# Retention with a Mish feed-forward layer: state products and scores on quarters of the TensorE array, in one stretch a visit

## The chip, the cores and the metric

The kernel runs on one core of a Trainium2 chip. The metric is the device time of one execution, in microseconds. A profile is of one execution; its span is the time from the first to the last instruction that the profiler saw on the core.

## What is computed

Eight batches of eight heads, 576 positions, head size 64. Each head is a masked product with decay, with no softmax; the heads are then put side by side and go through a two-layer network:

```python
scores = (1/sqrt(64)) * q @ k.T                   # [8, 8, 576, 576]
gamma  = 1 - 2.0 ** (-5 - head)
ret    = (scores * where(i >= j, gamma ** (i - j), 0)) @ v
x      = ret, heads side by side                  # [4608, 512]
h      = x @ w_in                                 # [4608, 2048]
out    = (h * tanh(softplus(h))) @ w_out          # [4608, 512], Mish between
```

## The kernel before

**Chunks and tiles.** The 576 positions of a batch are cut into chunks of 128 (c = 0 to 3) and one of 64; the 64-row ends of two batches make one chunk together (c = 4). The 36 chunks are taken four at a time: nine tiles of 512 tokens. Tiles 0 and 1 hold the chunks with c = 0, which need no state from earlier positions (the functions with f_). The other 28 chunks (numbers 8 to 35, N0 = 8) use the decay's recurrent form. In each:

- P (L271, VectorE) scales q, V (L276, GpSimd) scales v and makes vs; both round to bf16.
- T (L282) turns q and k into qkT, with eight TensorE transposes and a ScalarE copy for chunks below 18 (NPE), by a transposing transfer on SP's queue from 18 on.
- S (L294) makes the scores k q of the chunk with itself, eight matmuls with 64 rows of the array (one head each) and all 128 columns, into two PSUM banks (sc); VectorE multiplies by the causal mask and writes sm.
- state (L319) adds k times v of one chunk of one batch to the PSUM bank st, where the state of a batch is summed over c; VectorE copies it to ssb. Two heads lie above each other in 128 partitions, and the copy writes it twice, each time with the other head's half multiplied by zero (diag), so that the product can use all 128 rows. There are 32 states, in a fixed order; state_of says which one a chunk needs, done counts them, and a call of state makes the next one only if a chunk up to its argument needs it.
- O (L343, step_o) makes the chunk's result: eight products of ssb with q (L353; sixteen where c = 4, since the two 64-token ends need two batches' states) and eight outputs of vs with sm (L358), all of them with 64 columns of the array, added up in one bank (half of sc, or ops in tile 2). VectorE copies it to xT.

**The network.** g1(t, f) (L366 on) makes one of 16 slices of h for tile t: four matmuls of 512 columns at L371 into a bank hp, then Mish on ScalarE into gT. g2(t, i) makes a quarter of the sum of one 128-token result (four matmuls at L386, in a bank ops or hp); after four of them the result waits in ready until stores copies it (L422, VectorE) and sends it off on SP's queue.

**Order.** It is written out by hand, and every engine takes its instructions in program order. The loop over u (L529) runs g1 of tile 1 and the first half of its g2, with chunks 8 to 11 between; then the loop over t and i (L563) runs g1 of tile t and g2 of tile t-1 in turns (16 steps a tile), with two chunks' work in each block of eight steps, w = 0 to 7. In the trace a block shows two stretches of small matmuls: states and S at w = 0, states and O at w = 4. TensorE's last work is g2_last.

**Loads.** All loads are issued from GpSimd's queue (q, k, v with 256-byte runs; w_in and w_out in four loads each), in order with GpSimd's own operations; load (L253) is called by more_loads at w = 4 and 5, some seven chunks ahead of use. Buffers: qraw 5, vraw 7, qks 9, vs 5, sm 3, qkT 5, ssb 6. PSUM has eight banks: sc two times two, st one, hp two, ops one.

## Time and profile before

| | |
|---|---|
| median of three runs | 312.5 us (312.32, 312.5, 315.58) |
| the profiled execution | 313.61 us, span 311.9 us |
| granted TensorE clock | 1.0 of full speed |
| L371 and L386 of 128x512, mean of one | 380 and 379 ns from start to end |
| ScalarE Mish, L373, 128x512 | 598 ns |
| VectorE: sm L305, ssb L336, xT L362, res L422 | 1215, 685, 680, 688 ns |
| GpSimd: one load issue L263 (128 partitions), L267 (64) | 906 to 910, 706 to 745 ns |

TensorE busy, by stage:

| from, us | to, us | what runs | TensorE busy, us |
|---|---|---|---|
| 0 | 20 | first loads, tile 0's chunks | 13.7 of 20.0 |
| 20 | 50.8 | network of tile 0, tile 1's chunks | 30.5 of 30.8 |
| 50.8 | 80.3 | the loop over u | 29.2 of 29.5 |
| 80.3 | 107.2 | t = 2 | 26.6 of 26.8 |
| 107.2 | 262.5 | t = 3 to 7 | 154.2 of 155.3 |
| 262.5 | 294.7 | t = 8 | 32.1 of 32.3 |
| 294.7 | 311.9 | last quarters, store | 14.0 of 17.2 |

How to read it: "busy" counts a matmul from its start to its modelled end, and successive ones overlap; so the distance from start to start tells more than the duration. In a timeline the columns are start and duration in us, engine, line, operation, output and inputs, the array's rows and columns in use (128*64), the size, and how many were merged (x8); in square brackets, how long the engine had been idle and what ended it.

### The profile page before, as it was taken

The numbers are of one execution on the slowest core, as the hardware profiler recorded it, in microseconds if no ns is written. First come the engines' busy times: TensorE is split into PE (matmuls) and PEld (weight loads), VectorE is DVE, ScalarE is ACT, GpSimd is POOL, SyncE is SP. The second block draws the span as 40 slices with busy tenths as digits, with TensorE's granted clock in tenths as the row PEclk, the third lists the DMA queues.
The fourth block names the chain that finished last, engine by engine and source line by source line (L and its number), as shares of the span: only waits on it lengthen the run. The fifth ranks groups of instructions, "written<-read, shape, count | busy, mean of one in ns | idle before, by whom it ended". The sixth has DMA issues, their size and how long they took to land.

```text
span 311.9 us, 5809 instructions
## 1 busy us (share of the span) xinstructions
PE 300.3 (96%) x2429; PEld 152.3 (49%) x2468; DVE 137.1 (44%) x200; ACT 110.7 (36%) x183; POOL 143.6 (46%) x178
## 2 busy tenths in 40 slices
PE   7769999999999999999999999999999999999995
PEld 3444554555465554545454444545454544444444
DVE  4723455778637635443434453535354332001111
ACT  4546345671453623233333333232323333333300
POOL 8578849989985976274726262612010000000000
PEclk9999999999999999999999999999999999999999
DMA  7999999999995999999996949371504100010031
GB/s 177 234 206 205 220 208 221 256 171 175 232 203 96 148 181 191 155 195 146 179 178 116 189 88 218 77 144 37 101 36 101 36 34 36 35 34 34 36 101 68
DMA packets 73642, 42.85 MB, mean 137 GB/s; under 512 B 58640, under 2 KB 64528, under 8 KB 73616
## 3 DMA queue, kind: packets, MB, share of 16 engines
q0 software_dynamic: 48640, 27.27, 61.1%
q1 hardware_dynamic: 24832, 15.08, 23.3%
q8 instruction: 19, 0.31, 0.5%
q10 hardware_dynamic: 144, 0.13, 0.1%
q14 instruction: 7, 0.06, 0.1%
HBM read 38.80 MB, written 9.44 MB: 155 GB/s over the span
## 4 chain that ended last, share of the span: by engine, by line
PE 92%; issue 2%; DMA 2%; POOL 2%; DVE 0%; ACT 0%; POOLq 0%; ACTq 0%
PE hp L371 39%; PE ops L386 30%; PE hp L386 4%; PE sc L301 3%; PE st L333 3%; DMA gT<-in_v_dram 2%; PE hp L403 2%; PE sc L353 2%; PE sc L358 2%; PE sc L288 1%; PE st L403 1%; PE ops L403 1%; PE hp L414 1%; POOL gT L106 1%; POOL vb L222 1%
## 5 line engine op out<-in xcount | busy, mean ns | idle before, releaser
L371 PE MATMUL hp<-xT,w_in_t 128*128 128x512 bf16 (+1 forms) x562 | 141.3, 373 | 2.2 <-DVE xT L239 0.8
L373 ACT ACTIVATE gT<-hp 128x512 bf16<-128x512 f32 (+1 forms) x148 | 86.8, 586 | 156.4 <-PE hp L371 144.2
L386 PE MATMUL ops<-w_out_t,gT 128*128 128x512 bf16 x430 | 110.1, 379 | 0.4
L371 PEld LDWEIGHTS <-w_in_t 128*128 128x128 bf16 x592 | 55.1, 98 | 61.9 <-DVE xT L239 1.3
L386 PEld LDWEIGHTS <-gT 128*128 128x128 bf16 x496 | 48.2, 98 | 58.1 <-issue 0.8
L422 DVE COPY res<-ops 128x512 f32<-128x512 f32 x28 | 19.3, 688 | 82.7 <-PE ops L386 79.7
L279 POOL TENSOR_TENSOR vs<-vraw,gv 128x512 bf16<-128x512 f32 x28 | 30.3, 1096 | 51.8 <-PE sc L358 37.6
L336 DVE TENSOR_TENSOR ssb<-st,diag 128x512 bf16<-128x512 f32 x32 | 21.9, 685 | 47.2 <-PE st L333 47.2
L305 DVE TENSOR_TENSOR sm<-sc,mask 128x1024 bf16<-128x1024 f32 x28 | 33.0, 1215 | 6.2 <-PE sc L301 6.2
L263 POOL DMA_DIRECT2D qraw<-in_q_dram x24 | 21.8, 910 | 12.8 <-DVE qks L273 9.6
L263 POOL DMA_DIRECT2D vraw<-in_v_dram x24 | 21.8, 908 | 2.9 <-DMA vpair<-in_v_dram 1.5
L263 POOL DMA_DIRECT2D qks<-in_k_dram x24 | 21.8, 906 | 1.3 <-DMA w_out_t<-in_moe_w_out_dram 0.9
L273 DVE TENSOR_TENSOR qks<-qraw,gq 128x512 bf16<-128x512 f32 x28 | 20.2, 758 | 0.0
L362 DVE CAST xT<-sc 128x512 bf16<-128x512 f32 x24 | 15.3, 680 | 0.0
L386 PE MATMUL hp<-w_out_t,gT 128*128 128x512 bf16 x61 | 14.7, 379 | 0.2
L289 ACT COPY qkT<-sc 128x1024 bf16<-128x1024 bf16 x10 | 10.1, 1010 | 8.0 <-PE sc L288 8.0
L215 DVE TENSOR_TENSOR sm<-sc,dmask 128x1024 bf16<-128x1024 f32 x8 | 9.4, 1220 | 5.0 <-PE sc L211 5.0
L353 PE MATMUL sc<-qkT,ssb 128*64 128x128 bf16 (+1 forms) x224 | 9.5, 213 | 0.0
L358 PE MATMUL sc<-sm,vs 128*64 128x128 bf16 x192 | 9.4, 219 | 0.0
L301 PE MATMUL sc<-qkT 64*128 64x128 bf16 x224 | 9.0, 218 | 0.0
L403 PEld LDWEIGHTS <-gT 128*128 128x128 bf16 x64 | 5.8, 98 | 6.5
L267 POOL DMA_DIRECT2D qraw<-in_q_dram x8 | 5.6, 706 | 7.3 <-DVE qks L273 7.3
(103 smaller groups left out, 192.0 us busy)
## 6 DMA issues: line engine op xcount, KB each, us to landing
out_dram<-res SPq DMA_DIRECT2D x31, 256.0 KB, 3.0
qraw<-in_q_dram POOLq DMA_DIRECT2D x24, 256.0 KB, 6.0
vraw<-in_v_dram POOLq DMA_DIRECT2D x24, 256.0 KB, 6.8
qks<-in_k_dram POOLq DMA_DIRECT2D x24, 128.0 KB, 6.4
w_in_t<-in_moe_w_in_dram POOLq DMA_DIRECT2D x4, 512.0 KB, 11.1
w_out_t<-in_moe_w_out_dram POOLq DMA_DIRECT2D x4, 512.0 KB, 9.8
gT<-in_q_dram SPq DMA_DIRECT2D x4, 256.0 KB, 4.9
gT<-in_k_dram POOLq DMA_DIRECT2D x8, 128.0 KB, 6.3
```

Of the source, the lines that this page charges most:

```text
L263: nc.gpsimd.dma_start(out=t, in_=src[b, :, ds(P * c, P), :].rearrange("h p d -> p h d"))
L273: nc.vector.tensor_tensor(live[n]["qks"][:, 0], live[n]["q"], gq[:, c, :].unsqueeze(2).to_broadcast([P, H, D]), op=OP.mult)
L279: nc.gpsimd.tensor_tensor(vs, live[n]["v"], gv[:, c, :].unsqueeze(2).to_broadcast([P, H, D]), op=OP.mult)
L301: nc.tensor.matmul(sc[:, e, p, :], lhsT=qk[r, 1, p, :], rhs=qk[r, 0, p, :], start=True, stop=True)
L305: nc.vector.tensor_tensor(sm.rearrange("p e n i -> p (e n) i"), sc.rearrange("p e n i -> p (e n) i"), m.unsqueeze(1).to_broadcast([P, 2 * ...
L336: nc.vector.tensor_tensor(ssb.rearrange("p e n d -> p e (n d)"), st.rearrange("p n d -> p (n d)").unsqueeze(1).to_broadcast([P, 2, NP * 64 ...
L353: nc.tensor.matmul(ot[ds(64 * e, 64), p, ds(i0, iw)], lhsT=st_sb[bb, cc][:, e, p, :], rhs=qk[:, 0, p, ds(i0, iw)], start=(i0 == 0 and p == ...
L371: nc.tensor.matmul(hp[:, cols], lhsT=w_in_t[:, c, ts(f, P)], rhs=xts[t][:, c, cols], start=(c == 0), stop=(c == KC - 1))
L373: nc.scalar.activation(gts[t][:, f, cols], hp[:, cols], AX.Mish)
L386: nc.tensor.matmul(ops, lhsT=gts[t][:, f, ts(s, P)], rhs=w_out_t[:, f, :], start=(f == 0), stop=(f == nF - 1))
L403: nc.tensor.matmul(outs[0, s], lhsT=gts[0][:, f, ts(s, P)], rhs=w_out_t[:, f, :], start=(f == 0), stop=(f == nF - 1))
L422: copy(ot, ops)
```

## The change

- **Scores** use quarters of the array: each head's eight matmuls become sixteen, with 64 rows and 64 columns.
- **States** are copied to ssb once, without zeros (half on VectorE and half on ScalarE from tile 2 on, `two`), and their **products** use 64 rows and 64 columns too.
- So that a quarter's column half goes with a half of the heads, heads h and h+4 now lie above each other in xT, and the rows of w_in are taken in that order, with two loads of 64 partitions in place of each load of 128.
- **One stretch a visit**: two chunks are taken together. A visit makes a state, the outputs of both chunks, a further state, the products, and the scores of the next two chunks. The results lie in two banks, copied to xT by ScalarE and VectorE. A block of eight steps has one visit, at w = 6; the loop over u has a first stretch at u = 9 and visits at 15 and 22, where it had five stretches.
- From tile 3 on the order of g1 and g2 in four steps is g1 g1 g2, g2, g1 g2, g1 g2 (g2 first right after a visit).
- P, V and T come at other steps; for chunks from 18 on, P at w = 4 and 5, T at w = 7 and 0.
- **hold**: before GpSimd issues a block's loads, it copies one element a partition of the qkT of the two chunks whose transposing transfers came last, and so waits for them.

The diff, without its context and without the removed step_o (L343 to L362):

```diff
@@ -79,11 +79,12 @@
-    w_in_r = moe_w_in.rearrange("(c p) f -> p c f", p=P)
+    w_in_r = moe_w_in.rearrange("(a c r) f -> a r c f", a=2, r=64)
     def load_w_in(f0, n):
-        nc.gpsimd.dma_start(out=w_in_t[:, :, ds(f0, n)], in_=w_in_r[:, :, ds(f0, n)])
+        for a in range(2):
+            nc.gpsimd.dma_start(out=w_in_t[ds(64 * a, 64), :, ds(f0, n)], in_=w_in_r[a, :, :, ds(f0, n)])
@@ -156,11 +157,6 @@
-    diag = consts.tile([P, 2], F32)
-    nc.vector.memset(diag, 0.0)
-    nc.vector.memset(diag[0:64, 0:1], 1.0)
-    nc.vector.memset(diag[64:P, 1:2], 1.0)
@@ -231,11 +227,11 @@
-        for p in range(NP):
-            for e in range(2):
-                nc.tensor.matmul(ot[ds(64 * e, 64), p, :], lhsT=vb[:, 2 * p + e, :],
-                                 rhs=fst[t]["sm", b][:, 2 * p + e, :],
-                                 start=(p == 0), stop=True, skip_group_check=True)
+        for h in range(NP):
+            for a in range(2):
+                nc.tensor.matmul(ot[ds(64 * a, 64), h, :], lhsT=vb[:, NP * a + h, :],
+                                 rhs=fst[t]["sm", b][:, NP * a + h, :],
+                                 start=(h == 0), stop=True, skip_group_check=True)
@@ -297,9 +293,10 @@
         for p in range(NP):
             for e in range(2):
-                r = ds(64 * e, 64)
-                nc.tensor.matmul(sc[:, e, p, :], lhsT=qk[r, 1, p, :], rhs=qk[r, 0, p, :],
-                                 start=True, stop=True)
+                for a in range(2):
+                    r, j = ds(64 * e, 64), ds(64 * a, 64)
+                    nc.tensor.matmul(sc[j, e, p, :], lhsT=qk[r, 1, p, j], rhs=qk[r, 0, p, :],
+                                     start=True, stop=True, skip_group_check=True)
@@ -316,7 +313,7 @@
-    def state(upto):
+    def state(upto, two=False):
@@ -332,34 +329,65 @@
-        ssb = tr.tile([P, 2, NP, 64], BF16, name="ssb", bufs=6)
-        nc.vector.tensor_tensor(
-            ssb.rearrange("p e n d -> p e (n d)"),
-            st.rearrange("p n d -> p (n d)").unsqueeze(1).to_broadcast([P, 2, NP * 64]),
-            diag.unsqueeze(2).to_broadcast([P, 2, NP * 64]), op=OP.mult)
+        ssb = tr.tile([P, NP, 64], BF16, name="ssb", bufs=6)
+        if two:
+            nc.vector.tensor_copy(ssb[:, 0:2, :], st[:, 0:2, :])
+            nc.scalar.copy(ssb[:, 2:NP, :], st[:, 2:NP, :])
+        else:
+            nc.vector.tensor_copy(ssb, st)
-    def step_o(n):
...
+    def outputs(n, banks):
+        both = [pool.tile([P, 2, 2 * P], F32, name=name) for pool, name in banks]
+        for x in range(2):
+            sm, vs = live[n + x]["sm"], live[n + x]["vs"]
+            for h in range(NP):
+                for a in range(2):
+                    hh = NP * a + h
+                    nc.tensor.matmul(both[h % 2][ds(64 * a, 64), h // 2, ts(x, P)], lhsT=vs[:, hh, :],
+                                     rhs=sm[:, hh % 2, hh // 2, :],
+                                     start=(x == 0 and h < 2), stop=False, skip_group_check=True)
+        return both
+    def outputs_end(n, both):
         t, s = divmod(n, NCH)
+        for x in range(2):
+            assert done[0] > state_of[n + x]
+            b, c = chunks[n + x]
+            qk = live[n + x]["qk"]
+            for i0, iw, bb, cc in [(0, P, b, c - 1)] if c < 4 else [(0, 64, b, 3), (64, 64, b + 1, 3)]:
+                for h in range(NP):
+                    for a in range(2):
+                        e, p = h % 2, (NP * a + h) // 2
+                        r = ds(64 * e, 64)
+                        nc.tensor.matmul(both[e][ds(64 * a, 64), h // 2, ds(P * x + i0, iw)],
+                                         lhsT=st_sb[bb, cc][r, p, :], rhs=qk[r, 0, p, ds(i0, iw)],
+                                         start=False, stop=True, skip_group_check=True)
         if s == 0:
             xts[t] = xp.tile([P, KC, NCH * P], BF16, name="xT")
-        nc.vector.tensor_copy(xts[t][:, :, ts(s, P)], ot)
+        for e, copy in enumerate((nc.scalar.copy, nc.vector.tensor_copy)):
+            copy(xts[t].rearrange("p (h e) i -> p e h i", e=2)[:, e, :, ds(P * s, 2 * P)], both[e])
+    held = consts.tile([P, 2], BF16)
+    def hold(n):
+        nc.gpsimd.tensor_copy(held[:, n % 2:n % 2 + 1], live[n]["qk"][:, 1, NP - 1, P - 1:P])
+    def visit(n, banks, upto, two=False):
+        state(upto, two)
+        both = outputs(n, banks)
+        state(upto, two)
+        outputs_end(n, both)
+        for m in (n + 2, n + 3):
+            att(m, "S")
@@ -377,7 +405,7 @@
-            if (t == nT - 1 and s % 2) or (t == 1 and s < 2):
+            if (t == nT - 1 and s % 2) or (t == 1 and s == 0):
@@ -524,12 +552,13 @@
-    att(N0, "PV")
+    pv = {0: 0, 4: 1, 8: 2, 11: 3, 16: 4, 18: 5}
+    tp = {3: 0, 6: 1, 11: 2, 13: 3, 18: 4, 20: 5}
     for u in range(24):
         j, w = divmod(u, 4)
+        if u in pv:
+            att(N0 + pv[u], "PV")
...
-        elif w == 1 and j > 0:
-            if j > 3:
-                state(N0 + j - 1)
-            if j < 5:
-                att(N0 + j - 1, "S")
-            if j < 4:
-                state(N0 + j - 1)
-            if j > 1:
-                att(N0 + j - 2, "O")
-            if j == 4:
-                state(N0 + j - 1)
-            stores()
-        elif w == 2 and 0 < j < 5:
+        if u == 9:
+            state(N0 + 1)
+            att(N0, "S")
+            att(N0 + 1, "S")
+            state(N0 + 1)
+        elif u == 15:
+            visit(N0, ((ps_o, "ops"), (ps_h, "hp")), N0 + 3)
+            state(N0 + 3)
+        elif u == 22:
+            visit(N0 + 2, ((ps_h, "hp"), (ps_h, "hp")), N0 + 5)
+        if w == 2 and 0 < j < 5:
             f_state(1, j - 1, nc.vector)
-        elif (w == 3 and j < 5) or (w == 2 and j == 5):
-            att(N0 + j, "T")
+        if u in tp:
+            att(N0 + tp[u], "T")
         stores()
         if u < nF:
             g1(1, u)
@@ -560,41 +587,54 @@
+    last = n_chunks - 1
     for t in range(2, nT + 1):
         for i in range(nF):
             n, w = NCH * (t + 1) + i // 8 * 2, i % 8
-            if t in (3, 4) and i in (4, 12):
-                load_k0(2 * t - 2 + i // 8)
-            by_pe = n + 2 < NPE
-            if w == 0:
-                stores()
-                state(n + 1)
-                att(n, "S")
-                att(n + 1, "S")
-            if w == 4:
+            if w == 6 and n < n_chunks:
+                visit(n, ((ps_h, "hp"), (ps_h, "hp")), min(n + 4, last), True)
                 state(n + 3)
-                stores()
-                att(n, "O")
-                att(n + 1, "O")
-                state(n + 3)
-            if by_pe and w in (1, 3):
+            if w in (1, 3) and n + 2 < NPE:
                 att(n + 2 + w // 2, "P")
+            if w in (4, 5) and n + 4 >= NPE:
+                att(n + w, "P")
             if w in (0, 1):
                 att(n + 2 + w, "V")
+            if w == 4 and NPE <= n + 2 < n_chunks:
+                hold(n + 2)
+                hold(n + 3)
+            if w == 4 and t in (3, 4):
+                load_k0(2 * t - 2 + i // 8)
             if w in (4, 5):
                 more_loads(n + w - 2 + PF)
-            if w - (5 if by_pe else 0) in (0, 1):
-                att(n + 2 + (w == 1 or w == 6), "T")
+            if w in (2, 4) and n + 2 < NPE:
+                att(n + 1 + w // 2, "T")
             if w == 7 and n + 4 >= NPE:
-                att(n + 4, "P")
-                att(n + 5, "P")
+                att(n + 4, "T")
+            if w == 0 and n + 2 >= NPE:
+                att(n + 3, "T")
             stores()
-            if t < nT:
+            if t == 2:
+                if w == 6:
+                    g2(1, 8 + i // 2)
                 g1(t, i)
-            if t == 2:
-                if i % 2:
+                if i % 2 and w != 7:
                     g2(1, 8 + i // 2)
-            elif t < nT or i < 12:
+            elif t == nT:
+                if i < 12:
+                    g2(t - 1, i)
+            elif w == 6:
+                g2(t - 1, i)
+                g1(t, i)
+            elif i % 4 == 0:
+                g1(t, i)
+                g1(t, i + 1)
+                g2(t - 1, i)
+            else:
+                if i % 4 != 1:
+                    g1(t, i)
                 g2(t - 1, i)
```

More of the change, by code (lines that the diff above doesn't have):

```diff
@@ L340, in state @@
         st_sb[b, c] = ssb
         return True
-    def step_o(n):
-        b, c = chunks[n]
-        t, s = divmod(n, NCH)
-        assert done[0] > state_of[n]
-        qk, vs, sc, sm = (live[n][x] for x in ("qk", "vs", "sc", "sm"))
-        ot = ps_o.tile([P, NP, P], F32, name="ops") if t == 2 else sc[:, 0]
-        halves = [(0, P, b, c - 1)] if c < 4 else [(0, 64, b, 3), (64, 64, b + 1, 3)]
-        for i0, iw, bb, cc in halves:
-            for p in range(NP):
-                for e in range(2):
-                    nc.tensor.matmul(ot[ds(64 * e, 64), p, ds(i0, iw)], lhsT=st_sb[bb, cc][:, e, p, :],
-                                     rhs=qk[:, 0, p, ds(i0, iw)],
-                                     start=(i0 == 0 and p == 0), stop=False, skip_group_check=True)
-        for p in range(NP):
-            for e in range(2):
-                nc.tensor.matmul(ot[ds(64 * e, 64), p, :], lhsT=vs[:, 2 * p + e, :], rhs=sm[:, e, p, :],
-                                 start=False, stop=True, skip_group_check=True)
+    def outputs(n, banks):
[9 more added lines that the diff above has]
+        return both
@@ L433, in att @@
         for step in steps:
-            {"P": step_p, "V": step_v, "T": step_t, "S": step_s, "O": step_o}[step](n)
+            {"P": step_p, "V": step_v, "T": step_t, "S": step_s}[step](n)
     dve, act, pool = nc.vector.tensor_copy, nc.scalar.copy, nc.gpsimd.tensor_copy
@@ L524, in more_loads @@
                 queued[0] += 1
-    att(N0, "PV")
+    pv = {0: 0, 4: 1, 8: 2, 11: 3, 16: 4, 18: 5}
+    tp = {3: 0, 6: 1, 11: 2, 13: 3, 18: 4, 20: 5}
     for u in range(24):
         j, w = divmod(u, 4)
+        if u in pv:
+            att(N0 + pv[u], "PV")
         if w == 0 and j > 0:
-            att(N0 + j, "PV")
             if j < 5:
```

## The prediction

> **What bounds the kernel now.** I read the page first: busy time, the slices, the chain. Then the timeline of TensorE from one end to the other, those of VectorE, ScalarE and GpSimd around the places that the change touches, and the tile view of qkT.
>
> ```profile
> PE 300.3 (96%) x2429; PEld 152.3 (49%) x2468; DVE 137.1 (44%) x200; ACT 110.7 (36%) x183; POOL 143.6 (46%) x178
> ...
> PE   7769999999999999999999999999999999999995
> ...
> PE 92%; issue 2%; DMA 2%; POOL 2%; DVE 0%; ACT 0%; POOLq 0%; ACTq 0%
> ```
>
> TensorE is the end of the chain, and from 20 us on it never rests. So a change counts only through TensorE's own sequence, a new wait of TensorE, or the first 20 us. How that sequence is made up, from the timeline of TensorE:
>
> ```profile
> 113.22 1.03 PE L386 MATMUL ops<-w_out_t,gT 128*128 128x512 bf16 x4
> 114.18 0.32 PE L333 MATMUL st<-vs,qks 128*64 128x64 bf16 x8
> 114.33 0.39 PE L353 MATMUL sc<-qkT,ssb 128*64 128x128 bf16 x8
> 114.55 0.39 PE L358 MATMUL sc<-sm,vs 128*64 128x128 bf16 x8
> 114.78 0.39 PE L353 MATMUL sc<-qkT,ssb 128*64 128x128 bf16 x8
> 115.00 0.39 PE L358 MATMUL sc<-sm,vs 128*64 128x128 bf16 x8
> 115.28 0.32 PE L333 MATMUL st<-v0s,k 128*64 128x64 bf16 x8
> 115.53 1.04 PE L371 MATMUL hp<-xT,w_in_t 128*128 128x512 bf16 x3
> ...
> 121.58 1.03 PE L386 MATMUL ops<-w_out_t,gT 128*128 128x512 bf16 x4
> 122.54 0.32 PE L333 MATMUL st<-vs,qks 128*64 128x64 bf16 x8
> 122.78 0.62 PE L301 MATMUL sc<-qkT 64*128 64x128 bf16 x16
> 123.34 1.04 PE L371 MATMUL hp<-xT,w_in_t 128*128 128x512 bf16 x3
> ```
>
> The first number is the start. A dense group of four starts 0.864 us after the one before it (0.216 a matmul; call it a unit). Entering a stretch of small matmuls costs 0.10 (113.22 + 0.864 = 114.08, and the state starts at 114.18). A state takes 0.15, eight N=128 matmuls on half the array 0.22 (28 ns each), the switch from states to scores 0.09 (122.69 to 122.78), sixteen scores 0.45, leaving about 0.10.
>
> **The sum now.** From 50.81 (g1 of tile 1) to 305.08 (L414) are 254.3 us. Dense: 1008 matmuls x 0.216 = 217.8. Ten transposes at L288 of 0.47: 4.7. Four waits of 0.085 in the last tiles, where ops changes hands (267.72 and three more): 0.3. The other 31.4 are scores, states, products, outputs and switches: 6.0 up to 80.34 (the loop over u, and the first scores of tile 2), 25.4 behind it.
>
> **Quarters.** No row has a 64x64 matmul. Nearest is a run of N=64 on half the array:
>
> ```profile
> 99.14 0.42 PE L353 MATMUL sc<-qkT,ssb 128*64 128x64 bf16 x16
> 99.39 0.28 PE L358 MATMUL sc<-sm,vs 128*64 128x128 bf16 x4
> ```
>
> Sixteen pairs of weight load and matmul start within 0.25 us, 15.6 ns a pair: so fast can they be issued. Four tiles that each keep the 56 ns per matmul of the halves would give 14 ns. If the quarters ran only two at a time it would be 28 ns, the rows of L301 and L358; less than 14 is excluded, since each tile still streams its 128 columns. I take 15.6 for the sum and correct it at the end. Then the products of a chunk fall from 0.22 to 0.125, but the scores do not gain: two chunks are now 32 matmuls, 0.50 for 0.45. (A chunk with c = 4 has sixteen products, 0.25 still.)
>
> "TensorE: Matmul & The Clock Gate" of the Trainium skill, Part 1, says that matmuls never start closer than about 25 ns however small they are. The run above has 15.6 ns between starts on alternating halves, so I go by the measurement; by the page, some 670 quarter matmuls would cost 6.3 us more (an estimate) and the change would lose.
>
> **A visit.** Entry 0.10, state A 0.15, outputs of two chunks 0.45, state B 0.15, switch 0.09, products 0.25, scores 0.50, exit 0.10: 1.79. One wait is new: B writes the bank that A's copy still reads. VectorE starts 0.35 after A's first matmul (114.53 against 114.18). Half a copy is 128 columns: from the 0.688 and 0.424 of 512 and 256 columns on VectorE about 0.29, from 0.585 and 0.372 about 0.27 on ScalarE, side by side; 0.05 more to TensorE makes 0.69, while the outputs cover 0.60. So 0.10 of waiting, 1.89 in all; with whole copies on VectorE (two=False) 0.22. Today's pair of stretches averages 25.4 / 12 = 2.12.
>
> Twelve visits: 22.7. By the order of states three of them do a third state (0.15 and a switch back of 0.09): +0.7. The last has neither scores nor states: -0.9. Four chunks with c = 4: +0.5. Sum 23.0 for 25.4: **-2.4**.
>
> **The loop over u.** Six stretches become three: at u = 9 1.18, at u = 15 2.25 (with 0.22 and a third state), at u = 22 2.01; 5.4 for 6.0. Against it: at u = 15 VectorE gets, after the visit's start, two copies, the xT copy (0.68), two sm (2.35), a third copy, and only then P of chunk N0+4 (0.68). That ends some 5.5 us after the visit's start; TensorE reaches its transpose at 2.25 + 3 x 0.864 = 4.84. I book a wait of 0.75 there and 0.1 for N0+3 at u = 13, where the same queue ends just about in time. Net **+0.3**.
>
> **The first 20 us.** GpSimd's timeline:
>
> ```profile
> 6.36 0.77 POOL L86 DMA_DIRECT2D w_in_t<-in_moe_w_in_dram  x1
> 7.12 1.17 POOL L117 DMA_DIRECT2D gT<-in_v_dram  x1
> ...
> 9.60 2.24 POOL L86 DMA_DIRECT2D w_in_t<-in_moe_w_in_dram  x3
> 11.99 1.17 POOL L222 CAST vb<-gT 128x512 bf16<-128x512 f32 x2 [0.16 <-DMA gT<-in_v_dram]
> 17.67 0.87 POOL L222 CAST vb<-gT 128x512 bf16<-128x512 f32 x1 [4.51 <-DMA gT<-in_v_dram]
> ```
>
> Each w_in load becomes two of half the descriptors. An issue takes 0.52 to 0.56 for small ones (L106) and 0.69 to 0.75 for 64 partitions (L267); at 0.6, a load costs 1.2 for 0.76. Queued behind are the second v load (0.4 later) and the casts vb at 11.99 (1.2 later, as 0.4 vanishes in the wait before 8.97). The casts have slack: the second sm behind them ended at 16.6 and would end at 17.8, and the next link is the vb at 17.67, after 4.51 us of waiting for v, and TensorE stood still for 1.72 before it. So only v's landing counts. Its transfer queues behind v and w_in anyway (issued by 8.3, landed by 17.7). Bounds: 0 (a gain is excluded: nothing in that queue gets shorter), or the whole 0.7 of an issue; I take **+0.2**, nearer to 0. GB/s in the windows there is 204 to 256 for whole tiles.
>
> "SBUF — State Buffer" of the Trainium skill, Door 1, speaks against this split: 64 partitions reach half of the ports, 196 GB/s against 328 at 1 MiB, and two such loads serialize. An estimate by it is 1.1 us more for the first w_in load, and v behind it as much later. Our queue moves only about 204 GB/s with all 128 partitions, so I do not book that.
>
> **Orders, loads, transposes.** Pairs g1 g1 g2 g2 give the copy of ops a unit more: the four waits of 0.085 go, **-0.3**. Both hp banks of a visit were last written 1.73 before it (0.86 in tile 2), the 0.60 of L373 fits; after it, two copies of 0.6 to 0.7 are covered by scores and g2 (1.36). From chunk 18 on the transposing transfers are asked for seven and six steps before their scores, where it was eight and seven:
>
> ```profile
> DMA to landing us min/median/max: 3.1/6.0/11.8
> ```
>
> Six steps of two units and the visit's own 1.29 before the scores are 11.7 us: enough but in the worst case seen. P now comes in steps 4 and 5 instead of 7; on VectorE the visit's copies queue behind it, but its q was asked for a block earlier, and L273 shows no wait at all for q. On SP the stores queue behind a transposing transfer; SP idles 223 us waiting for res, and there are four res buffers. The new wait (hold) sits on GpSimd, a one-column copy (0.1 by the smallest rows there). Behind it queue two loads (six issues of 0.9) and the next V; the q that is loaded is wanted some 1.5 blocks (over 20 us) later, against 3.1 to 11.8 of landing. Cost 0; if the cover went, R2 below. ScalarE gets 1.1 us of copies a visit and is busy 36% now. Removing diag frees 0.2 of VectorE at the start, off the chain.
>
> **Sum.** -2.4 + 0.3 - 0.3 + 0.2 = -2.2 at 15.6 ns; about 670 quarter matmuls at 14 ns make it -3.3. I take -3.0, nearer to the second, since at N=128 the halves keep exactly the 56 ns. The profiled execution of 313.6 (span 311.9) becomes 310.6; it lies 1.1 above the median of 312.5, so the median becomes **309.5**.
>
> **Rivals.**
> *R1, slower: quarters run two at a time.* For: no row shows four tiles at once. Against: 15.6 ns of issue. At 28 ns 670 x 12.4 ns = 8.3 more than -2.2: 318.6. It decides from 18.9 ns a pair (2.2 / 670 above 15.6), and is over 1% slower from 23.5. Chance 0.12.
> *R2: scores wait for a transposing transfer, or loads come late behind hold.* Every transfer at 13 instead of 6 us gives 1.3 us in nine visits: 11.7, less the gain of 3.0: 321.2; half of that wait 315.3. The median of 6.0 speaks against it. Chance 0.05.
> *R3: no wait that I booked exists, at 14 ns.* Visits of 1.71, loop -0.6, start 0: -5.6, 306.9. Chance 0.10.
> *R4: VectorE gives the gain back.* With 0.3 instead of 0.1 in each of twelve visits (2.4) and 1.5 instead of 0.85 in the u loop (0.65): 3.1 above the forecast, 312.6. For it: up to six VectorE operations now queue in one visit. Chance 0.13.
> The forecast itself, 307.5 to 311.5, has 0.60.
>
> **Numbers.** A difference of 1% (3.1 us) is about what a measurement of this kernel can tell. The forecast lies on that edge: half of its 0.60 is faster. Faster 0.30 + 0.10 = 0.40; slower 0.17 from R1 and R2; the rest 0.43. The range goes from R3's 306.9 to 315.0, which leaves out most of R1 and half of R2.
>
> **What would show it.** TensorE's timeline: stretches of 1.8 to 2.0 us, L-lines of products and scores with starts 14 to 16 ns apart; a gap before the second state of about 0.1; a gap before the transpose at u = 18; vb's second wait ending by 18. It is wrong if the quarter matmuls start over 19 ns apart, if scores wait for qkT, or if v lands over 1 us later.

## The result, and the profile after

The median went from 312.52 to 317.41 us (six runs of each, 312.30 to 315.58 and 317.28 to 317.86): slower by 1.4%, ratio 1.0144, 95% interval 1.0109 to 1.0179. The forecast was 309.5, and its range ended at 315.0. The profiled execution took 317.86 us, span 316.2, 4.3 more than before. Here and below a median takes all executions of a kernel and a ratio leaves out those more than 1.5% above its fastest, so that the two need not agree.

The page of the changed kernel: busy time, the chain by engine, and three groups (busy us, mean ns of one, idle time before them and what ended it):

```profile
PE 299.4 (95%) x2692; PEld 150.7 (48%) x2692; DVE 121.4 (38%) x183; ACT 124.1 (39%) x219; POOL 149.9 (47%) x200
...
PE 87%; DVE 3%; issue 3%; POOL 2%; DMA 2%; ACT 1%; DVEq 0%; POOLq 0%; ACTq 0%
...
L381 POOL COPY held<-qkT 128x1 bf16<-128x1 bf16 x18 | 3.7, 205 | 59.9 <-DMA qkT<-qks 59.9
...
L335 ACT CAST ssb<-st 128x128 bf16<-128x128 f32 x22 | 5.9, 266 | 26.6 <-DVE ssb L334 26.6
```

TensorE is busy 0.9 us less than before, yet the span grew: work was saved, and waits came in (3.6 us of them in eleven visits, for the copies to ssb). VectorE, ScalarE and GpSimd together now hold 6% of the chain, where they had 2%. Where the 4.3 us lie, from the starts of the same work in TensorE's timelines:

| stage | before, us | after, us | difference | forecast |
|---|---|---|---|---|
| start to the second half of tile 0's first g1 | 20.03 | 22.62 | +2.6 | +0.2 |
| from there to the loop over u | 30.78 | 30.78 | 0 | 0 |
| the loop over u, to the first g1 of tile 2 | 29.53 | 30.76 | +1.2 | +0.3 |
| the rest | 231.6 | 232.0 | +0.5 | -2.7 |

In the rest, the last tiles gained 0.34 (they run without the four gaps of 0.085), and the visits lost 0.8. One visit without a third state, in the timeline of TensorE, VectorE and ScalarE (A and B are its first and second state):

```profile
137.81 0.32 PE L330 MATMUL st<-vs,qks 128*64 128x64 bf16 x8
...
137.96 0.62 PE L352 MATMUL hp<-sm,vs 128*64 128x128 bf16 x16
...
138.17 0.29 DVE L334 CAST ssb<-st 128x128 bf16<-128x128 f32 x1 [1.55 <-PE st L330]
138.55 0.27 ACT L335 CAST ssb<-st 128x128 bf16<-128x128 f32 x1 [1.76 <-DVE ssb L334]
...
138.96 0.32 PE L330 MATMUL st<-vs,qks 128*64 128x64 bf16 x8 [0.38 <-ACT ssb L335]
...
139.20 0.42 PE L369 MATMUL hp<-qkT,ssb 64*64 64x128 bf16 x16
...
139.45 0.62 PE L298 MATMUL sc<-qkT 64*64 64x128 bf16 x32
...
140.00 0.60 PE L414 MATMUL ops<-w_out_t,gT 128*128 128x512 bf16 x2
```

The quarters do what was reckoned: sixteen products from 139.20 to 139.45, with nothing lost at the switch to the scores (15.6 ns each), and the 32 scores in about 0.45 (14 ns). But the halves of state A's copy run one behind the other. VectorE's is done at 138.46, ScalarE's starts at 138.55 and ends at 138.82, and state B waits for it until 138.96, 1.15 after A's first matmul. The outputs were through at about 138.41 (0.45 after 137.96), so TensorE lost 0.55 here.

The start, in the timelines of GpSimd (issues of loads count as its work) and TensorE:

```profile
12.53 0.61 POOL L87 DMA_DIRECT2D w_in_t<-in_moe_w_in_dram  x1 [0.55 <-DMA gT<-in_v_dram]
13.93 0.61 POOL L87 DMA_DIRECT2D w_in_t<-in_moe_w_in_dram  x1 [0.79 <-DMA w_in_t<-in_moe_w_in_dram]
14.54 1.18 POOL L218 CAST vb<-gT 128x512 bf16<-128x512 f32 x2
20.27 0.86 POOL L218 CAST vb<-gT 128x512 bf16<-128x512 f32 x1 [4.55 <-DMA gT<-in_v_dram]
...
21.19 0.41 PE L232 MATMUL st<-sm,vb 128*64 128x128 bf16 x8 [1.75 <-POOL vb L218]
```

Two of the eight issues waited until an earlier load had landed. Counted in the program, each of the two waited for the load eight places before it in GpSimd's own order. So the first two casts start at 14.54 for 11.99, and the first outputs of tile 0 (L232) at 15.22 for 12.66, after 2.96 us in which TensorE did nothing. The third cast, which waits for v to land, starts at 20.27 for 17.67, and TensorE waits for it once more (1.75, as the 1.72 before). In the loop over u one gap stands out, in the timelines of VectorE and TensorE:

```profile
74.69 1.35 DVE L269 TENSOR_TENSOR qks<-qraw,gq 128x512 bf16<-128x512 f32 x1
...
76.09 0.62 PE L284 MATMUL sc<-ident,qks 128*128 128x128 bf16 x8 [1.36 <-DVE qks L269]
```

P (L269) stands behind the visit's copies and masks on VectorE, as was expected, but it also takes 1.35 us, where the median of its 28 is 0.68.

### The profile page after: what moved, and what is told of

It reads as the page before. It is cut to its first block, busy times and chain, and to the rows that moved or that the text cites. A ratio compares the mean times of both kernels' runs of the same rounds, so it can differ in the third digit from the quotient of the medians.

```text
span 316.2 us, 6365 instructions
## 1 busy us (share of the span) xinstructions
PE 299.4 (95%) x2692; PEld 150.7 (48%) x2692; DVE 121.4 (38%) x183; ACT 124.1 (39%) x219; POOL 149.9 (47%) x200
## 4 chain that ended last, share of the span: by engine, by line
PE 87%; DVE 3%; issue 3%; POOL 2%; DMA 2%; ACT 1%; DVEq 0%; POOLq 0%; ACTq 0%
PE hp L399 39%; PE ops L414 31%; PE st L330 3%; PE hp L414 3%; DMA w_in_t<-in_moe_w_in_dram 2%; PE hp L431 2%; PE sc L298 2%; PE sc L284 2%; PE hp L369 1%; PE st L431 1%; PE ops L431 1%; PE hp L442 1%; DVE ssb L334 1%; ACT ssb L335 1%; DVE sm L302 1%
## 5 line engine op out<-in xcount | busy, mean ns | idle before, releaser
L399 PE MATMUL hp<-xT,w_in_t 128*128 128x512 bf16 (+1 forms) x592 | 137.3, 373 | 0.9 <-DVE xT L235 0.8
L414 PEld LDWEIGHTS <-gT 128*128 128x128 bf16 x496 | 47.4, 98 | 56.0
L381 POOL COPY held<-qkT 128x1 bf16<-128x1 bf16 x18 | 3.7, 205 | 59.9 <-DMA qkT<-qks 59.9
L259 POOL DMA_DIRECT2D qraw<-in_q_dram x24 | 22.0, 916 | 2.9 <-DMA vpair<-in_v_dram 1.5
L334 DVE CAST ssb<-st 128x128 bf16<-128x128 f32 x22 | 6.4, 292 | 42.6 <-PE st L330 42.6
L269 DVE TENSOR_TENSOR qks<-qraw,gq 128x512 bf16<-128x512 f32 x28 | 22.1, 804 | 1.6 <-DMA qraw<-in_q_dram 1.6
L335 ACT CAST ssb<-st 128x128 bf16<-128x128 f32 x22 | 5.9, 266 | 26.6 <-DVE ssb L334 26.6
L375 DVE CAST xT<-hp 128x512 bf16<-128x512 f32 x14 | 9.7, 692 | 4.5 <-PE hp L369 3.9
L330 PE MATMUL st<-vs,qks 128*64 128x64 bf16 x192 | 7.6, 200 | 2.6 <-ACT ssb L335 2.5
L330 PEld LDWEIGHTS <-qks 128*64 128x64 bf16 x192 | 5.1, 110 | 9.3 <-issue 8.0
L375 ACT CAST xT<-hp 128x512 bf16<-128x512 f32 x13 | 7.7, 590 | 4.2 <-PE hp L369 4.2
```

Source lines behind the costliest of these rows:

```text
L259: nc.gpsimd.dma_start(out=t, in_=src[b, :, ds(P * c, P), :].rearrange("h p d -> p h d"))
L269: nc.vector.tensor_tensor(live[n]["qks"][:, 0], live[n]["q"], gq[:, c, :].unsqueeze(2).to_broadcast([P, H, D]), op=OP.mult)
L330: nc.tensor.matmul(st[ds(64 * e, 64), p, :], lhsT=ks[:, 2 * p + e, :], rhs=vs[:, 2 * p + e, :], start=(c == 0 and p == 0), stop=True, skip ...
L375: copy(xts[t].rearrange("p (h e) i -> p e h i", e=2)[:, e, :, ds(P * s, 2 * P)], both[e])
L399: nc.tensor.matmul(hp[:, cols], lhsT=w_in_t[:, c, ts(f, P)], rhs=xts[t][:, c, cols], start=(c == 0), stop=(c == KC - 1))
L414: nc.tensor.matmul(ops, lhsT=gts[t][:, f, ts(s, P)], rhs=w_out_t[:, f, :], start=(f == 0), stop=(f == nF - 1))
```

## The experiments

Theory: three separate waits make the loss, each on TensorE's path. The halved copies are serial (about 3.5 us), the w_in loads in eight pieces delay the casts (2.6), and P of chunk N0+4 stands behind the visit on VectorE (1.4). Rivals: the 64 partitions of each load slow the transfers; hold delays work that matters; quarters cost time at the scores. Each ratio is to runs of the kernel before on the same chip, whose median was 312.6 to 313.4 us; unless said otherwise, an edit is to the changed kernel.

**Each wait alone.** whole_copy:

```diff
-                visit(n, ((ps_h, "hp"), (ps_h, "hp")), min(n + 4, last), True)
+                visit(n, ((ps_h, "hp"), (ps_h, "hp")), min(n + 4, last))
```

> The changed kernel, but from tile 2 on each state is copied to ssb whole on VectorE, not half on VectorE and half on ScalarE. In the trace of the changed kernel the ScalarE half starts only when the VectorE half has ended (26.6 us of waiting in 22 copies), so a visit's second state starts some 0.55 after the outputs are issued. Theory (the two halves run one after the other, and this is most of what a visit lost): one copy of 0.42 ends 0.32 earlier than the pair, eleven visits make 3.5 us: 313.9. Rival (VectorE or ScalarE is late for another reason, or the wait is hidden elsewhere): within 0.5 of 317.4.

315.18 us, ratio 1.0025 (0.9987 to 1.0064): below the changed kernel by 2.2 by the medians and by 3.7 by the ratios, where 3.5 was expected. TensorE's timeline of its profiled execution:

```profile
137.23 0.32 PE L330 MATMUL st<-vs,qks 128*64 128x64 bf16 x8 [0.17 <-DVE ssb L337]
```

State A had started at 136.30, so B now starts 0.93 after it, for 1.15. A whole copy on one engine is sooner done than two halves on two. That execution took 320.0 us: the scores at 221.19 waited 3.46 us for a transposing transfer, and the granted clock was 0.50 from 222 to 224. No scores waited so in the changed kernel's own profile.

p_early:

```diff
-    pv = {0: 0, 4: 1, 8: 2, 11: 3, 16: 4, 18: 5}
+    pv = {0: 0, 4: 1, 8: 2, 11: 3, 14: 4, 18: 5}
```

> The changed kernel, but P and V of chunk N0+4 come at u = 14, ahead of the visit at u = 15, instead of u = 16. Theory (the transpose at u = 18 waits 1.36 us because P queues on VectorE behind the visit's copies and masks): the gap goes, 1.2 to 1.5 us less, about 316.0. Rival (P waits for its q to land, or for GpSimd): the gap stays, 317.4; or P now delays the copies of the visit's states, and the time goes there.

316.32 us, ratio 1.0076 (1.0043 to 1.0108), below the changed kernel by 1.1 by the medians and 2.1 by the ratios, and the gap at u = 18 is gone: the transposes start at 74.02 without a wait.

**The start.** Two kernels put one half of the suspected cost into the kernel before. before_halves splits by partitions, as the change does, before_columns by columns, with all 128 partitions:

```diff
-        nc.gpsimd.dma_start(out=w_in_t[:, :, ds(f0, n)], in_=w_in_r[:, :, ds(f0, n)])
+        for a in range(2):
+            nc.gpsimd.dma_start(out=w_in_t[ds(64 * a, 64), :, ds(f0, n)], in_=w_in_r[ds(64 * a, 64), :, ds(f0, n)])
...
+        for a in range(2):
+            nc.gpsimd.dma_start(out=w_in_t[:, :, ds(f0 + 256 * a, 256)], in_=w_in_r[:, :, ds(f0 + 256 * a, 256)])
```

> The kernel before, with one edit: each w_in load is two loads of 64 partitions, rows in the old order. Theory A (the start's 2.6 us come from loading w_in in halves): the second vb cast that waits for v moves from 17.7 to about 20.2 us, time 315.1. Rival B (they come from the new order of the rows, or from other work in the start): 312.5 to 313.1, where 0.6 is the later issue of v.

> The kernel before, with one edit: each w_in load is two loads of 256 columns with all 128 partitions, so as many loads and issues as in halves. Theory A1 (loads of 64 partitions are moved more slowly, and v behind them lands late): v lands at most 0.6 later, by the later issue; time 312.5 to 313.1. Theory A2 (the number of loads does it, by their issues and by waiting for earlier ones to land): as with halves, about 315.

316.5 us, ratio 1.0074 (1.0036 to 1.0113), and 315.38 us, ratio 1.0019 (0.9981 to 1.0057). In the profiles the first casts start at 14.38 and 14.11 for 11.99, and the second half of g1 2.1 and 1.8 us later than in the kernel before. So twice the loads, split either way, hold the casts back by over 2 us. With columns no issue waits for a landing: six take 4.48, where six of 64 partitions take 3.7 and wait 1.2. The share of the 64 partitions stays open: 0.3 by the two profiles, 1.1 by the medians, and the interval of before_columns includes no loss at all. casts_first puts the first two casts ahead of the last six issues:

```diff
+    for b in range(2):
+        vb = first.tile([P, H, D], BF16, name="vb", bufs=4)
+        nc.gpsimd.tensor_copy(vb, v0[b])
+        fst[0]["vb"][b] = vb
     for i in range(1, 4):
         load_w_in(512 * i, 512)
...
-    for b in range(3):
-        f_v(0, b, pool)
+    f_v(0, 2, pool)
```

> The changed kernel, but GpSimd casts the first two v tiles (vb) ahead of issuing the last three w_in loads, now six issues. Theory (the start's loss comes from GpSimd's order: the casts stand behind six issues, the last two of which wait until an earlier load has landed, eight loads before each): the casts start at 12.0 to 12.3 instead of 14.5, the second half of g1 at 20.0 to 20.8 instead of 22.6; 1.8 to 2.6 us less, 314.8 to 315.6. Rival (v's landing at 20.2 limits, since loads of 64 partitions move slowly): the casts come earlier, but the third one stays at about 20 and the time at 317.4.

315.76 us, ratio 1.0057 (1.0003 to 1.0111). GpSimd's timeline:

```profile
12.65 1.16 POOL L149 CAST vb<-gT 128x512 bf16<-128x512 f32 x2 [3.01 <-DMA gT<-in_v_dram]
```

The second half of g1 starts at 20.06, as it did in the kernel before (20.03), and the profiled span is 2.6 shorter than the changed kernel's (313.6). So GpSimd's order makes the loss, but the edit moves two things: the casts come sooner (TensorE waits 1.20 for them, not 2.96), and six loads of w_in come later, with v landing sooner (third cast at 17.71, not 20.27). The profile of p_early, whose start is the changed kernel's, helps to tell them apart. TensorE's timeline, and the windows view (from and to, length, busy time of TensorE, its weight loads, VectorE, ScalarE and GpSimd; the granted clock, 1.00 at full speed; DMA share, GB/s):

```profile
14.94 0.96 PE L232 MATMUL hp<-sm,vb 128*64 128x128 bf16 x16 [3.00 <-POOL vb L218]
...
16.00:18.00 2.00, 2.00 (x19) 1.01 (x16) 1.20 (x2) 0.52 (x1) 0.97 (x2) 0.50 1.26 204
```

There v is early (third cast at 17.03), and the second half of g1 still starts at 22.12: behind the wait for the first casts TensorE runs at half its clock. before_halves and before_columns have such a stretch too (0.50 from 16 to 18 and 0.52 from 18 to 20), so their 2.1 and 1.8 include it.

**What turned out free, and what did not.** no_hold leaves out both calls of hold (it computes nothing that the output needs). scores_halves makes the scores as the kernel before did:

```diff
-            if w == 4 and NPE <= n + 2 < n_chunks:
-                hold(n + 2)
-                hold(n + 3)
...
-                for a in range(2):
-                    r, j = ds(64 * e, 64), ds(64 * a, 64)
-                    nc.tensor.matmul(sc[j, e, p, :], lhsT=qk[r, 1, p, j], rhs=qk[r, 0, p, :],
-                                     start=True, stop=True, skip_group_check=True)
+                r = ds(64 * e, 64)
+                nc.tensor.matmul(sc[:, e, p, :], lhsT=qk[r, 1, p, :], rhs=qk[r, 0, p, :],
+                                 start=True, stop=True)
```

> The changed kernel without hold: loads are issued without waiting for the transposing transfers. Theory (GpSimd's 60 us of waiting in hold lie beside other work, and the scores have 11.7 us for a transfer): no difference in the time, within 0.5 of 317.4. Rival 1 (hold keeps the transfers from landing late): some land over 12 us after their issue, and the scores of those visits wait, 1 us or more in total. Rival 2 (hold itself puts the loads beside the next transfers: median to landing 8.1 us with it, 6.0 before): the median falls back to 6 to 7.

> The changed kernel with the scores on halves again: sixteen matmuls of 64 rows and 128 columns for two chunks in place of 32 on quarters. Theory (quarters start 14 ns apart and halves 28, so the scores gain nothing by quarters but the switch of the array's division behind the products): each visit is 0.05 to 0.10 longer, 0.7 to 1.2 us in all, 318.1 to 318.6. Rival (32 issues cost more than 16): 0.5 us or more faster than 317.4.

no_hold: 317.77 us, ratio 1.0159 (1.0122 to 1.0197), no gain. The transposing transfers landed 4.3 us after they were asked for, at the median, instead of 8.1, so it is hold that makes them late (so too 4.5 in combo_whole_free below for 8.0 in combo_whole), and nothing waited for them. scores_halves: 318.81 us, ratio 1.0217 (1.0153 to 1.0282), an interval that overlaps the changed kernel's. By the rows the quarters' scores do not cost but save a little, since the switch from products to scores takes 0.35 with halves (139.34 to 139.69) and 0.25 with quarters, the products' own time included.

**The second state behind the scores.** state_last moves state(upto, two) behind the scores, with the copies still halved:

```diff
         both = outputs(n, banks)
-        state(upto, two)
         outputs_end(n, both)
         for m in (n + 2, n + 3):
             att(m, "S")
+        state(upto, two)
```

> The changed kernel, but a visit's second state comes behind the scores, not between the outputs and the products; copies to ssb in halves as in the changed kernel. Theory (the wait for the first state's copies, 0.45 to 0.55 from the end of the outputs to the second state, is what the visits lost): the stretch is 1.85 to 1.95 instead of 2.24, eleven visits give 3.3 to 4.3 us, 313.1 to 314.1. Rival (the copies or the banks hold up the products or the next g1 as well): the stretch stays over 2.1 and the time over 316.

332.35 us, ratio 1.0619 (1.0584 to 1.0654): a miss. TensorE's waits, in us in all, times and longest:

```profile
PE st L330 <- ACT ssb L335: 8.8, 3, 3.0
```

VectorE's half of B's copy now stands in its queue behind the two masks (2.35 us), ScalarE's half behind VectorE's, Mish behind ScalarE's half, and the next state behind both. That is the serial pair again, at a worse place. The 8.8 and 2.8 more for a copy on VectorE do not make up the 15 us alone: behind each of these four waits the granted clock is at 0.50 to 0.58 for 2 us or more (0.50 from 130 to 134).

**All three together.** combo_whole joins casts_first, p_early and whole_copy; combo_whole_free also leaves hold out; combo_scalar_last has the second state behind the scores and copies it whole on ScalarE, the first and third on VectorE:

```diff
-        state(upto, two)
+        state(upto)
         both = outputs(n, banks)
-        state(upto, two)
+        if not two:
+            state(upto)
         outputs_end(n, both)
         for m in (n + 2, n + 3):
             att(m, "S")
+        if two:
+            state(upto, True)
...
         if two:
-            nc.vector.tensor_copy(ssb[:, 0:2, :], st[:, 0:2, :])
-            nc.scalar.copy(ssb[:, 2:NP, :], st[:, 2:NP, :])
+            nc.scalar.copy(ssb, st)
```

> The changed kernel with the three repairs together: two casts of v ahead of the last three weight loads, step P of chunk N0+4 at u=14 instead of 16, and the state copied whole by VectorE. Theory (three separate waits, each on TensorE's path and independent of each other): each alone took 1.7 (casts first), 1.1 (step P) and 2.2 us (whole copy) off the changed kernel's 317.4, the sum is 312.4 by these medians and 311.3 by what the waits were worth in the trace (2.6 + 1.2 + 2.3); I take 311.8, just below the kernel before, with the steady visits 1.5 to 2.0 us each below the kernel before's length not regained: state B still waits 0.15 to 0.25 us in each. Rival (the gains overlap, since a later start leaves slack further on): 314 to 315.

> As combo_whole, without the hold before the transposing transfers' products. Theory (the hold costs nothing and only makes the transfers land later): the same within 0.4 us, 311.4 to 312.2, the transfers landing 3 to 4 us sooner at the median. Rival (with less slack on TensorE the late transfers now end the scores' wait): 1 us or more below combo_whole.

> The changed kernel with the casts of v first and step P at u=14, and in t=2 to 8 the second state behind the scores, its copy whole on ScalarE (about 0.37 us), the first and third states' whole on VectorE. Theory (the loss of the run with the second state last came from its copy queueing on VectorE behind the two masks of 2.35 us; ScalarE has nothing as long ahead of it than the xT copy of 0.59): TensorE waits for no copy of the second state inside a visit, a visit without the third state shrinks from about 2.25 to 1.95 us, 310 to 311. Rival (any copy put on ScalarE holds up Mish, and with it the next products of the 128x512 kind): 314 or more, with g1's second-next group waiting for ScalarE.

| kernel | median (lowest), us | ratio to before, 95% interval |
|---|---|---|
| combo_whole | 312.31 (311.32) | 0.9979, 0.9939 to 1.0019 |
| combo_whole_free | 312.12 (311.57) | 0.9966, 0.9931 to 1.0001 |
| combo_scalar_last | 311.90 (311.19) | 0.9952, 0.9911 to 0.9993 |

The gains add up: 311.8 was expected of combo_whole, 312.31 came. Leaving out hold changed nothing again. combo_scalar_last was expected at 310 to 311 and missed that by 0.9. Its visit has the 1.73 us from A to the next group that the theory asked for (137.71 to 139.44), but the third state waited for B's copy on ScalarE, 0.6 at worst.

combo_scalar_third lets the third state wait for the next step; combo_v_first is that with load_first_v(2) ahead of the first load_w_in:

```diff
                 visit(n, ((ps_h, "hp"), (ps_h, "hp")), min(n + 4, last), True)
+            if w == 7 and n < n_chunks:
                 state(n + 3)
```

> As combo_scalar_last, with the third state of a visit one group of products later (two groups of 1.73 us at most), so that it finds its copy done. Theory (all that is left in the steady visits is that wait, about 0.6 us at four visits, and the switch to one more stretch costs about 0.25 less what is spared): the step between visits with a third state shrinks from 16.5 to 16.0 to 16.2, the other steps stay at 15.66; t=2 to 8 is 1.2 to 2.0 us shorter, 310.3 to 311 where the kernel before is at 312.5 to 313.3. Rival (a stretch of its own costs what it saves): no difference to combo_scalar_last, 311.9.

> As combo_scalar_third, with the load of the second pair of v ahead of the first two weight loads instead of behind them. Theory (the late start of some executions is this load's landing, behind the weights in the queues): the third cast at 17 us or before in every profile, the second half of g1 at 19.6 to 20.1, the spread of the times smaller, the median 0.5 to 1.5 us below combo_scalar_third. Rival (the weight loads, now 1.2 us later, end the wait of the first g1 instead): the first g1 starts later by up to 1 us and the time is the same.

combo_scalar_third: 312.62 us (lowest 309.77), ratio 0.9947 (0.9908 to 0.9985). A visit of its profiled execution (309.77 us, span 308.1), in TensorE's timeline:

```profile
132.88 0.32 PE L334 MATMUL st<-vs,qks 128*64 128x64 bf16 x8
133.02 0.62 PE L355 MATMUL hp<-sm,vs 128*64 128x128 bf16 x16
133.57 0.42 PE L372 MATMUL hp<-qkT,ssb 64*64 64x128 bf16 x16
133.82 0.62 PE L302 MATMUL sc<-qkT 64*64 64x128 bf16 x32
134.36 0.32 PE L334 MATMUL st<-vs,qks 128*64 128x64 bf16 x8
```

No wait is left inside. From the outputs of one visit to those of the next there are 16 groups of 0.864, 13.82, and the visit:

| kernel | without a third state, us | with one, us |
|---|---|---|
| before (two stretches) | 16.0 | 16.2 to 16.3 |
| the change | 16.03 to 16.13 | 16.3 to 16.4 |
| whole_copy | 15.8 to 15.9 | 16.0 to 16.1 |
| combo_scalar_last | 15.66 | 16.4 to 16.5 |
| combo_scalar_third | 15.66 | 16.00 |

The step expected of it came out (16.0, 15.66), but not the median of 310.3 to 311: its twelve times lie from 309.77 to 320.33. combo_v_first narrowed the spread (310.24 to 315.22), but not to a better median: 312.49 us, ratio 0.9967 (0.9937 to 0.9997). In its profile the first g1 waited 2.57 us for w_in, as its rival had it, only more.

**Why the halves are serial.** Two kernels add twelve pairs of copies behind the changed kernel's end, VectorE and ScalarE 128 columns each. banks_probe, with pr one tile of two banks:

```diff
+        if i % 3 == 0:
+            nc.vector.tensor_copy(pv0[:, 0, 0, :], pr[:, 0, 0, :])
+            nc.scalar.copy(pv0[:, 1, 0, :], pr[:, 0, 2, :])
+        elif i % 3 == 1:
+            nc.vector.tensor_copy(pv0[:, 0, 0, :], pr[:, 0, 0, :])
+            nc.scalar.copy(pv0[:, 1, 0, :], pr[:, 1, 2, :])
+        else:
+            nc.vector.tensor_copy(pv0[0:64, 0, 0, :], pr[0:64, 0, 0, :])
+            nc.scalar.copy(pv0[64:P, 1, 0, :], pr[64:P, 0, 2, :])
```

> The changed kernel with twelve pairs of copies behind its end, four of each kind: VectorE and ScalarE each copy 128 columns out of (a) one bank of PSUM, (b) two banks, (c) one bank, but 64 partitions each. Nothing else is changed, and the time is only the old one plus the tail. Theory (two engines that read one bank are put one behind the other): (a) in series, ScalarE's starts when VectorE's has ended, (b) side by side, both starting within 0.1 us of each other. Rival (the order in the visits comes from something else, ScalarE's own queue or the ssb tile that both write): (a) starts side by side as (b) does. (c) has no forecast: in series if the bank alone counts, side by side if the partitions count too.

All three kinds ran in series, the pairs out of two banks too, against the theory:

```profile
315.59 0.29 DVE L651 CAST sm<-sc 128x128 bf16<-128x128 f32 x1 [0.54 <-PE sc L644]
315.91 0.27 ACT L652 CAST sm<-sc 128x128 bf16<-128x128 f32 x1 [0.56 <-DVE sm L651]
```

tiles_probe therefore changes the tiles: two tiles of PSUM into one of SBUF (a), one of PSUM into two of SBUF, out of two banks (b) or out of one (c).

```diff
+            nc.vector.tensor_copy(one[:, 0, 0, :], pr[1][:, 1, 0, :])
+            nc.scalar.copy(one[:, 1, 0, :], pr[0][:, 1, 2, :])
...
+            nc.vector.tensor_copy(one[:, 0, 0, :], pr[1][:, 0, 0, :])
+            nc.scalar.copy(two[:, 1, 0, :], pr[1][:, 1, 2, :])
...
+            nc.vector.tensor_copy(one[:, 0, 0, :], pr[1][:, 1, 0, :])
+            nc.scalar.copy(two[:, 1, 0, :], pr[1][:, 1, 2, :])
```

> The changed kernel with twelve pairs of copies behind its end again, VectorE and ScalarE 128 columns each, four of each kind: (a) out of two tiles of PSUM into one tile of SBUF, (b) out of one tile of PSUM, two banks, into two tiles of SBUF, (c) out of one tile of PSUM, one bank, into two tiles of SBUF. The pairs of the run before all read one tile and wrote one tile. If the tile that is read decides: (a) side by side, (b) and (c) in series. If the tile that is written decides: (a) in series, (b) and (c) side by side. If only one bank in one tile counts: (c) alone in series. The copies into xT, out of two tiles of PSUM into one tile, overlap in the visits, so I expect the first.

L651 and L652 are the copies of kind (a), L654 and L655 of kind (b):

```profile
316.88 0.27 ACT L652 CAST sm<-sc 128x128 bf16<-128x128 f32 x1
317.73 0.29 DVE L651 CAST sm<-sc 128x128 bf16<-128x128 f32 x1 [1.05 <-PE sc L646]
318.70 0.29 DVE L654 CAST sm<-sc 128x128 bf16<-128x128 f32 x1 [0.68 <-PE sc L646]
319.08 0.27 ACT L655 CAST sm<-sc 128x128 bf16<-128x128 f32 x1 [1.93 <-DVE sm L654]
```

In (a) ScalarE does not wait for VectorE, which comes first in the program, and even goes before it, its data being ready sooner. In (b) it waits, and so it does in (c). The tile that is read decides, not the bank, the partitions or the tile that is written. By the trace each second copy is released by the first, and starts 0.03 to 0.09 us behind its end. Such releases are inferred from the program's semaphore events, so this looks like an order that the program keeps; whether both could read at once without it was not tried. So the copies of xT, out of two tiles, overlap in every visit (139.70 on VectorE, 139.87 on ScalarE), and the halves of st never do.

## Why the prediction was wrong

**The visits (-2.4 forecast, +0.8 came).** The clause that failed is that the halves run "side by side". In series they let state B start 1.15 after A, not 0.69, and the wait is 0.55 in the visit shown (0.40 to 0.56 in all eleven), not 0.10. A visit without a third state takes about 16.07 - 13.82 = 2.25 for 1.89; eleven visits make 4.0 (the last has no second state). A term on the good side was also mis-sized: the sixteen products of a chunk with c = 4, booked at 0.5 in all, cost next to nothing (a visit's 24 products take 0.26, 155.25 to 155.51, where its usual sixteen take 0.25). That leaves 3.5, and 3.2 came. The other terms held: a visit less its wait is 1.70, where 1.79 was forecast at 15.6 ns and 1.71 at 14, and VectorE starts 0.36 after A (0.35). Of the 0.22 for whole copies whole_copy shows 0.33 (0.93 less the 0.60 of the outputs). The page "PSUM — Partial Sum Buffer" of the Trainium skill, section "PSUM bank collisions raise a hardware error", says that the compiler's scheduler adds a dependency between two engines that touch the same bank in the same 32 partitions, reads too, and that other banks or other such groups of partitions do not collide. The rows agree for halves of one bank (22 of 22 in series), but other banks or other partitions of the same tile did not help here, where the page would let them run at once.

**The first 20 us (+0.2 forecast, +2.6 came).** Two terms failed. "1.2 later" for the casts was 2.55: six issues took 3.7 where three took 2.24, and two waits for landings came on top. The trace of before was not searched for such waits: there the loads of qks and vraw wait 0.91 and 1.54 us, at 40.62 and 43.05, for w_out_t and vpair. And v's landing, booked at 0.2, came 2.6 later in this profile, which is a sign of being wrong that the prediction itself had named. "The casts have slack ... only v's landing counts" fits this one profile, where v ends TensorE's last wait. It does not fit the others: in five of seven further profiles with the same start the third cast begins at 17.03 to 17.36, sooner than in the kernel before, and the second half of g1 still at 22.12 to 22.79. There TensorE idles 3.0 to 3.3 us for the first casts, and the clock falls to half. So the late casts alone bring about what was lost; no term and no rival had a clock that drops. What was said against the rule of "SBUF — State Buffer", Door 1, is not shown: the third cast starts at 19.77 with 64 partitions and at 18.43 with columns, which is the rule's way, but it moved by more than that between executions with one order of issues (last section).

**The loop over u (+0.3 forecast, +1.2 came).** The mechanism and its place were right, the size was not. The three stretches took 1.18, 2.21 and 1.97, 5.4 as reckoned. P of chunk N0+4 began 4.85 after the visit's start, as reckoned too, but took 1.35 for 0.68, so that the wait was 1.5 from start to start for 0.75; why P took so long was not traced. At u = 13 it was 0.2 for 0.1. p_early, which moves P ahead of the visit, took the gap out.

**The last tiles (-0.3), hold (0), the transposing transfers.** Right: -0.34, no_hold level, no wait for qkT in the profile of the change. Two executions of other variants did wait for one transfer (3.46 and 2.0 us), so the cover that was reckoned is thin.

**The rivals.** R1 is refuted by the rows (14 to 15.6 ns), R2 by no_hold. R3's rate of 14 ns came for the scores, not for the products of 128 columns. R4 named the right kind of loss in the visits and the loop, 3.1 above the forecast, where 4.1 came (3.2 and 0.9); but in the visits its cause is a chain of two engines, not VectorE's queue, and the start is in none of the rivals.

**Where the expected gain went.** Into the three waits, in most profiles with half the clock behind that for the first casts. They can be taken out: the profiled execution of combo_scalar_third, the fastest of its twelve, has 309.77 us, where 310.6 was forecast for the profiled one. A gain over the kernel before is not shown, though: the ratio says 0.5%, with an interval that ends just below 1, and the medians of all executions (312.62 and 313.05) are level.

## What to carry to other kernels

Splitting a copy over two engines helped here only where the two read different PSUM tiles; look for a pair of readers of one tile in the trace before you book them side by side. Splitting a load costs an issue and, with many loads under way, a wait for an earlier landing: list what stands behind it in that queue, and follow each of these to TensorE before calling it slack. A wait of TensorE of two or three us can cost more than itself: look at the granted clock behind it. When a stretch of work is pulled together, sum up the queue of the engine that serves it, for the next step behind it pays.

## What was not expected of the hardware

**The clock drops after a short idle.** In combo_whole's profiled execution v landed so late that TensorE waited 3.85 us for the first casts, to 15.83. The windows view:

```profile
14.00:16.00 2.00, 0.17 (x4) 0.17 (x6) 0.00 (x0) 0.00 (x0) 0.84 (x2) 0.75 0.98 168
16.00:18.00 2.00, 2.00 (x33) 1.47 (x32) 0.69 (x1) 0.58 (x1) 2.00 (x4) 0.50 0.41 46
```

For 4 us the clock was 0.50, and the scores behind the outputs took 1.03 us for 0.62. The profiles have nineteen waits of TensorE between 1.99 and 3.85 us, and behind seventeen the clock was at about half for 2 us or more (behind 1.99 in combo_whole_free: 0.50 from 122 to 124); not behind the 2.96 of the change and the 2.57 of combo_v_first. None of 1.75 or less at the same place, before tile 0's outputs, did it. "TensorE: Matmul & The Clock Gate" of the Trainium skill, Part 1, tells of a free-running window of about 3.4 us whose phase differs from run to run, and of half the clock after at least one idle window. The phase would fit that 2.96 stayed without effect and 2.87 did not; but most of the seventeen waits were shorter than that window, so by these runs less idle time is enough. The clock is also the likeliest reason, though only argued, why the times of the repaired kernels spread: in combo_scalar_third the four executions with a mean granted clock of 1.0 took 309.8 to 310.7 us, the four at 0.989 and less 312.9 to 320.3.

**The start depends on when v lands.** The third cast started at 17.15 us in combo_scalar_third's profile, at 19.93 in that of combo_scalar_last and at 21.52 in that of combo_whole, with the same order of issues, and between 17.03 and 20.87 in the eight profiles with the changed kernel's start. What makes it late in some executions stays open; so does whether the limit of eight loads under way is the queue's or the program's, which was not tried.
